# Sparse attention and a squared-ReLU MoE on one core: casting DMAs for batches 2 and 3, earlier hooks, late strided x through DRAM

## Chip, cores, metric

One NeuronCore of a Trainium2 chip. The metric is device microseconds (us) of one execution; medians are over the executions of one kernel. Times in a profile count from the start of the profiled execution's span, which is 1.5 to 2 us shorter than the reported time. "Batch" is one of 8 attention batches, "chunk" one of 9 blocks of 512 tokens of the MoE, "group" one step of the program's schedule: mostly four or eight large matmuls. A DMA is *issued* when an engine puts it into its queue, and has *landed* when its data are there; the *granted clock* is the share of TensorE's full clock in the profile's clock records. A run is called slow when it is over 1.5% above the fastest of its kernel; ratios use the other, fast, runs alone.

## The reference

```python
def _attn_ref(q, k, v):                       # q, k, v: (8, 8, 576, 64) float32
    scores = scale * np.matmul(q, k.transpose(0, 1, 3, 2))
    rel = pos[:, None] - pos[None, :]
    mask_local = (rel >= 0) & (rel < 32)                                    # heads 0..3
    mask_strided = (rel >= 0) & (pos[None, :] % 32 == pos[:, None] % 32)    # heads 4..7
    ...                                       # masked softmax
    return np.matmul(attn, v)

def _moe_ref(x, w_in, w_out):                 # x: (4608, 512), w_in: (512, 2048), w_out: (2048, 512)
    r = np.maximum(x @ w_in, 0.0)
    return (r * r) @ w_out

def reference(**kwargs):
    ...
    x = np.ascontiguousarray(attn_out.transpose(0, 2, 1, 3)).reshape(B * S, H * D)
    return _moe_ref(x=x, **moe_kwargs)
```

## The kernel before

The kernel writes the order of every engine's instructions itself. A list of MoE groups is walked through; before each group come as many attention steps as are due, then the *hooks* of that group: loads, casts and DMA transposes. A hook only gives the place of an instruction in its own engine's queue. Each engine then runs its queue in order, waiting only where data or buffers make it wait.

Batches 0 and 1 load with casting DMAs on GpSimd's queue, straight to bf16. Batches 2 and 3 load float32 on SyncE's queue and GpSimd casts. From batch 2 on, q and k of the strided heads (`q_d`, `k_d`) go by a casting DMA to DRAM and come back through a DMA transpose on SyncE's queue (`qT_s`, `kT_s`). From batch 4 on, the local heads' q and k are transposed by DMA too (`qT`, `kTl`).

```python
    def cast_str_dram(b):
        for name, src in (("q", q), ("k", k)):
            t = dram.tile([4 * SP_, NJ * D], BF16, name=f"{name}_d")
            nc.gpsimd.dma_start(
                out=t.rearrange("(x y) c -> x (y c)", x=16),
                in_=src[b, H // 2:H].rearrange("h (x y) d -> (h x) (y d)", x=4))
            big[b, name] = t

    def transpose_str(b):
        for name in "qk":
            o = strT.tile([128, NJ // 2, 4 * SP_], BF16, name=f"{name}T_s")
            nc.sync.dma_start_transpose(out=o, in_=big.pop((b, name)))
            ...

    def transpose_local(u):
        ...
            nc.sync.dma_start_transpose(out=dst.rearrange("c (t p) -> c t p", p=QL),
                                        in_=s[name].rearrange("p t h d -> p (t h d)"))

    def load_v_str_sw(b):          # strided v by one casting DMA, rows of 1024 bytes: not used before
        t = v_st.tile([SP_, 2, NJ * D], FP32, name="v_st")
        t = t.rearrange("p h c -> p (h c)").bitcast(BF16).rearrange("p (h c) -> p h c", h=4)
        nc.gpsimd.dma_start(out=t, in_=v[b, 4:8].rearrange("h (p j) d -> p h (j d)", j=NJ))
        ...

    def loads(b):                  # batches 2 and 3
        u = 4 * b
        for i in range(2):
            load_qk_local(u + i, nc.sync, gate=gates.get(b) if i == 0 else None)
        for i in range(2):
            load_v_local(u + i, nc.sync)
        load_v_str(u + 2, nc.sync)
        load_v_str(u + 3, nc.sync)
        if b >= XB:
            cast_str_dram(b)
        cast_qk_local(u, pool2)    # pool2: copies on GpSimd
        cast_qk_local(u + 1, pool2)
        cast_v_local(u)
        cast_v_local(u + 1)
        cast_v_str(u + 2)
        cast_v_str(u + 3)

    def plan(b, n0, g0, g1):
        if b < LB:                 # LB = 4
            at(n0, lambda: loads(b))
            if b >= XB:            # XB = 2
                at(n0 + (12 if b == 2 else 6), lambda: transpose_str(b))
            return
        g = g0 + (g1 - g0) * 45 // 100
        at(g, lambda: loads_qk(b))
        at(max(g + 8, g0 + (g1 - g0) * 8 // 10), lambda: transpose_str(b))
        at(n0, lambda: loads_v(b))
        for i in range(2):
            at(g + 14 + 4 * i, lambda u=4 * b + i: transpose_local(u))
    ...
    for n, g in enumerate(groups):
        while done < due[n]:
            steps[done]()
            done += 1
        for fn in hooks.get(n, ()):
            fn()
        g()
        tick()
```

The softmax here doesn't subtract the row's maximum and nothing guards it: scores larger than these inputs give would overflow.

## Time and profile before

| | before |
|---|---|
| time, median of 4 runs | 319.46 us (318.58 to 319.88) |
| span of the profiled execution | 317.8 us |
| TensorE busy | 299.0 us, 94% of the span |
| TensorE waits for a DMA over 0.5 us | none |
| granted TensorE clock | full throughout |

The main views (busy times, slices, windows by stage, TensorE's waits) are in the prediction. This is SyncE's queue in the timeline of the kernel before (start in us, time until the queue went on, line, operation, tiles):

```profile
60.09 3.31 SPq L171 DMA_TRANSPOSE kT_s<-k_d  x1
...
64.60 0.39 SPq L118 DMA_DIRECT2D q_st<-in_q_dram  x1
...
99.15 1.20 SPq L198 DMA_TRANSPOSE kTl<-k_l  x1
```

The first is batch 2's second strided transpose; the trace has it landed at 66.2 us, 6.1 us after its issue. Batch 3's first load follows it **in the same queue**, 4.5 us later. So before the change the order of the queue kept the next batch's float32 loads behind most of this transpose; what kept GpSimd's own copies of that batch back is shown below. The third is the first transpose of batch 4's local k: it is out at 99 us, while chunk 3, beside which batch 4 is worked, has its first relu square at 118.5 us.

### The profile page before, as it was taken

To read this page: it belongs to the slowest core of one execution; us is meant where nothing else is said; L and a number is where in the kernel's file an instruction comes from. 1 tells how busy PE (TensorE), PEld (TensorE's weight loads), DVE (VectorE), ACT (ScalarE), POOL (GpSimd) and SP (SyncE) were. 2 spreads that over 40 slices of the span, in tenths; PEclk is the share of its full clock that TensorE was granted. 3 is DMA by queue.
4 is the path that set the end of the run, shared out by engine and by line. 5 is a ranking of instruction groups with operands and counts; after the bars stand their busy time and mean duration, and the time that the engine had idled before them with its cause. 6 is when DMAs were issued, how large, how long until landed. Compare 5 with 4: busy or idle time off the path is not lost.

```text
span 317.8 us, 6089 instructions
## 1 busy us (share of the span) xinstructions
PE 299.0 (94%) x2319; PEld 147.7 (46%) x2362; DVE 162.1 (51%) x398; ACT 164.5 (52%) x339; POOL 82.7 (26%) x108
## 2 busy tenths in 40 slices
PE   7899699989899989999999999999999999999994
PEld 2543354445455444444444444544454444444441
DVE  5366653668656975756565557564465222222200
ACT  3757455777546765554555455545543344444311
POOL 8653113726730714642074034000000000000000
PEclk9999999999999999999999999999999999999999
DMA  8999969999997999999599775100421000000121
GB/s 157 176 206 204 189 111 251 217 268 223 210 174 170 196 215 175 215 219 203 130 223 240 149 185 93 40 24 26 54 71 48 35 33 35 33 33 35 54 78 66
DMA packets 87052, 43.41 MB, mean 137 GB/s; under 512 B 72112, under 2 KB 79984, under 8 KB 86832
## 3 DMA queue, kind: packets, MB, share of 16 engines
q1 hardware_dynamic: 73520, 31.86, 46.0%
q0 software_dynamic: 13504, 11.17, 23.2%
q8 instruction: 18, 0.29, 0.4%
q14 instruction: 10, 0.08, 0.1%
HBM read 37.08 MB, written 12.98 MB: 157 GB/s over the span
## 4 chain that ended last, share of the span: by engine, by line
PE 87%; DVE 5%; ACT 3%; issue 3%; POOL 1%; ACTq 0%; DVEq 0%; POOLq 0%
PE ph L472 35%; PE py L495 27%; PE ph L495 10%; PE pt L333 4%; PE pt L418 4%; ACT r L478 2%; PE pt L448 1%; DVE g_sb L481 1%; DVE xt L456 1%; PE pt L495 1%; ACT e L343 1%; DVE kTl L299 1%; PE pt L284 1%; PE pt L321 1%; PE pt L394 1%
## 5 line engine op out<-in xcount | busy, mean ns | idle before, releaser
L472 PE MATMUL ph<-xt,w_in_b 128*128 128x512 bf16 x549 | 141.4, 379 | 3.3 <-DVE xt L456 1.9
L478 ACT ACTIVATE r<-ph 128x512 bf16<-128x512 f32 x141 | 84.0, 598 | 100.5 <-PE ph L472 96.8
L481 DVE TENSOR_TENSOR g_sb<-r 128x512 bf16<-128x512 bf16 x144 | 67.6, 472 | 105.5 <-ACT r L478 105.0
L495 PE MATMUL py<-w_out_b,g_sb 128*128 128x512 bf16 x380 | 99.7, 379 | 1.6 <-issue 0.6
L495 PEld LDWEIGHTS <-g_sb 128*128 128x128 bf16 x576 | 52.8, 98 | 60.5 <-issue 3.1
L472 PEld LDWEIGHTS <-w_in_b 128*128 128x128 bf16 x576 | 51.6, 98 | 54.0 <-issue 0.8
L343 ACT ACTIVATE e<-pt 72x288 bf16<-72x288 f32 (+1 forms) x128 | 47.9, 407 | 14.4 <-PE pt L333 14.2
L495 PE MATMUL ph<-w_out_b,g_sb 128*128 128x512 bf16 x154 | 37.4, 379 | 0.3
L418 PEld LDWEIGHTS <-e 128*128 128x128 bf16 (+1 forms) x384 | 20.1, 97 | 15.4 <-issue 1.9
L217 POOL CAST vl<-vl_st 128x768 bf16<-128x768 f32 x12 | 10.8, 900 | 48.6 <-DMA vl_st<-in_v_dram 27.7
L431 DVE TENSOR_TENSOR x_s<-pt,rinv 72x384 bf16<-72x384 f32 (+1 forms) x36 | 18.3, 509 | 1.2
L431 DVE TENSOR_TENSOR x_l<-pt,rinv 96x384 bf16<-96x384 f32 x32 | 17.7, 553 | 1.1
L430 DVE RECIPROCAL rinv<-pt 96x6 f32<-96x6 f32 (+2 forms) x68 | 12.5, 184 | 10.6 <-PE pt L418 10.4
L349 DVE TENSOR_TENSOR e<-e,mask_str 72x576 bf16<-72x576 bf16 x28 | 14.7, 526 | 5.9 <-ACT e L343 5.6
L140 POOL CAST q_l<-q_st 96x768 bf16<-96x768 f32 x12 | 11.0, 917 | 25.0 <-DMA q_st<-in_q_dram 24.9
L499 ACT COPY y<-py 128x512 f32<-128x512 f32 x25 | 14.6, 586 | 4.0 <-PE py L495 4.0
L349 DVE TENSOR_TENSOR e<-e,mask_full 128x576 bf16<-128x576 bf16 x28 | 14.0, 501 | 1.6 <-ACT e L343 1.5
L499 ACT COPY y<-ph 128x512 f32<-128x512 f32 x10 | 5.8, 584 | 17.1 <-PE ph L495 17.1
L249 POOL CAST vs<-v_st 72x1024 bf16<-72x1024 f32 x12 | 13.7, 1159 | 1.2 <-DMA v_st<-in_v_dram 0.9
L140 POOL CAST k_l<-k_st 96x768 bf16<-96x768 f32 x12 | 11.2, 933 | 10.0 <-DMA k_st<-in_k_dram 7.6
L418 PE MATMUL pt<-vs,e 72*128 72x65 bf16 x192 | 11.7, 193 | 1.1 <-ACT e L343 1.1
L418 PE MATMUL pt<-vl,e 128*128 128x65 bf16 x192 | 10.8, 193 | 0.0
(100 smaller groups left out, 168.9 us busy)
## 6 DMA issues: line engine op xcount, KB each, us to landing
out_dram<-y SPq DMA_DIRECT2D x36, 256.0 KB, 2.2
vl_st<-in_v_dram SPq DMA_DIRECT2D x24, 144.0 KB, 2.9
v_st<-in_v_dram SPq DMA_DIRECT2D x12, 288.0 KB
q_st<-in_q_dram SPq DMA_DIRECT2D x16, 144.0 KB, 8.2
k_st<-in_k_dram SPq DMA_DIRECT2D x16, 144.0 KB, 5.1
w_out_b<-in_moe_w_out_dram POOLq DMA_DIRECT2D x4, 512.0 KB, 14.9
q_d<-in_q_dram POOLq DMA_DIRECT2D x6, 288.0 KB, 5.0
k_d<-in_k_dram POOLq DMA_DIRECT2D x6, 288.0 KB, 6.5
```

The costliest lines, as they stand in the source:

```text
L140: copy(t.rearrange("p j h d -> p h j d"), s[name + "f"].rearrange("p h (j d) -> p h j d", j=6))
L249: (copy or nc.gpsimd.tensor_copy)(t[:, :, 0:D], s["vf"].rearrange("p h (j d) -> p (h j) d", d=D))
L333: nc.tensor.matmul(pss[row][half][0:kn, w * i:w * (i + 1)], lhsT, rhs, start=u > 3, stop=True, skip_group_check=u < 4)
L343: nc.scalar.activation(e[0:kn, lo:lo + S // 2], pss[row][half][0:kn, 0:S // 2], AF.Exp, scale=scale)
L349: nc.vector.tensor_tensor(x, x, m, op=ALU.mult)
L418: nc.tensor.matmul(po[:, n - n0, :], e[0:kn, pos(n):pos(n) + 128], rhs[0:kn, src(n), 0:D + 1], start=True, stop=True)
L431: nc.vector.tensor_tensor(x, po[0:w, 0:m, 0:D], rinv[0:w, 0:m].to_broadcast([w, m, D]), op=ALU.mult)
L472: nc.tensor.matmul(ph, w_in_b[:, kk, 128 * ff:128 * (ff + 1)], xt[kk][:, 512 * c:512 * (c + 1)], start=(kk == order[0]), stop=(kk == order ...
L478: nc.scalar.activation(r, ph, AF.Relu)
L481: later(1, lambda: nc.vector.tensor_tensor(g[:, ff, :], r, r, op=ALU.mult))
L495: nc.tensor.matmul(py, g[:, ff, 128 * j:128 * (j + 1)], w_out_b[:, ff, :], start=(ff == 0), stop=(ff == 15))
L499: nc.scalar.copy(y, py)
```

## The change

The intent: load batches 2 and 3 as batches 0 and 1 are, without GpSimd's casts; queue batch 1's reorders two to four groups sooner; finish each batch's attention two groups before its chunk (14 for batches 6 and 7), so that the MoE does not wait for x; take the strided x of batches 6 and 7 through DRAM and a DMA transpose instead of TensorE; and halve the last block.

```diff
     XB = 2
+    XD = B - 2
@@ step_E
+        if not local and b >= XD:
+            xd = dram.tile([S, 2 * D], BF16, name="x_d")
+            nc.sync.dma_start(out=xd.rearrange("(p j) c -> p (j c)", j=NJ), in_=x.rearrange("p n d -> p (n d)"))
+            nc.sync.dma_start_transpose(out=xt[p][:, b * S:(b + 1) * S], in_=xd)
+            st.pop(u)
+            return
@@ mm2: last block in two halves of 256 columns
+        if c == NCH - 1 and j == 3:
+            ...
@@ loads
     def loads(b):
-        u = 4 * b
-        for i in range(2):
-            load_qk_local(u + i, nc.sync, gate=gates.get(b) if i == 0 else None)
         ... (float32 loads and GpSimd's casts, all removed)
+        load_qk_local_sw(b, (4 * b, 4 * b + 1))
+        cast_str_dram(b)
+        load_v_local_sw(b)
+        for u in (4 * b + 2, 4 * b + 3):
+            t = vss[v_slot(u)]
+            h = 2 * units[u][1]
+            for i in range(2):
+                nc.gpsimd.dma_start(out=t[:, NJ * i:NJ * (i + 1), 0:D],
+                                    in_=v[b, h + i].rearrange("(p j) d -> p j d", j=NJ))
+            st.setdefault(u, {})["v"] = t
@@ schedule
-    ready = {2: 56}
+    ready = {2: 58, **{b: starts[b] - (14 if b >= XD else 2) for b in range(3, B)}}
@@ plan
-            if b >= XB:
-                at(n0 + (12 if b == 2 else 6), lambda: transpose_str(b))
+            at(g0, lambda: transpose_str(b))
+            for i in range(2):
+                at(g1 + 2 * i, lambda u=4 * b + i: cast_qk_local(u, dve2, "q"))
+                at(g1 + 2 * i + 1, lambda u=4 * b + i: cast_qk_local(u, dve2, "k"))
             return
-        g = g0 + (g1 - g0) * 45 // 100
+        g = 50 if b == LB else g0 + (g1 - g0) * 45 // 100
@@ hooks
-    second(12, lambda: cast_qk_local(4, dve2, "q"))
-    second(13, T_(4, "q"), lambda: cast_qk_local(4, dve2, "k"))
     ...
+    second(10, lambda: cast_qk_local(4, dve2))
+    second(11, lambda: cast_qk_local(5, dve2))
     ...
-    plan(2, 18, 0, 0)
+    plan(2, 14, 28, 28)
-    plan(3, 34, 0, 0)
+    plan(3, 38, 48, 45)
```

Cut: weights of groups, order of steps within a batch (`stream_steps`), exponentials at once beside chunk 1's second layer, PSUM banks of chunk 0's first groups, `vl_st`'s memsets moved to group 50. With `g = 50` the loads of batch 4 come at group 50 instead of 42, and its local transposes (`g + 14`, `g + 18`) at groups 64 and 68 instead of 56 and 60.

More of the change, by code (lines that the diff above doesn't have):

```diff
@@ L260 @@
     clock = [0]
+    relaxed = [False]
     pending = []
@@ L468, in mm1 @@
         if kks[0] == order[0]:
-            phs[ff] = banks["pt"].pop(0) if pool == "pt" else bank(pool or "ph")
+            phs[ff] = banks["pt"].pop(0) if pool == "pt" else bank(pool[:2] if pool else "ph")
         ph = phs[ff]
@@ L479, in mm1 @@
         if c == 0 and 2 < ff < NP:
-            banks["pt"].insert(0, ph)
+            banks["pt"].append(ph)
         later(1, lambda: nc.vector.tensor_tensor(g[:, ff, :], r, r, op=ALU.mult))
@@ L487, in mm2 @@
         g = gs[c]
+        if c == NCH - 1 and j == 3:
+            if part % 2:
+                return
+            cols = slice(128 * part, 128 * part + 256)
+            py = bank(pool)[:, 0:256]
+            for ff in range(16):
+                nc.tensor.matmul(py, g[:, ff, 128 * j:128 * (j + 1)], w_out_b[:, ff, cols],
+                                 start=(ff == 0), stop=(ff == 15))
+            y = y_pool.tile([128, 512], FP32, name="y")
+            nc.scalar.copy(y[:, 0:256], py)
+            r0 = 512 * c + 128 * j
+            nc.sync.dma_start(out=out[r0:r0 + 128, cols], in_=y[:, 0:256])
+            return
         if part == 0:
@@ L505 @@
     T_ = lambda u, nm: (lambda: step_T(u, nm))
-    S_ = lambda u, at_once=False: (lambda: step_S(u, at_once))
+    S_ = lambda u, at_once=False: (lambda: step_S(u, at_once or relaxed[0]))
     D_ = lambda u, part: (lambda: step_D(u, part))
@@ L542, in stream_steps @@
     def stream_steps(lo, hi, base):
-        order = [T_(lo, "q"), T_(lo, "k"), T_(lo + 1, "q"), S_(lo), T_(lo + 1, "k")]
+        order = [T_(lo, "q"), T_(lo, "k"), T_(lo + 1, "q"), S_(lo), T_(lo + 1, "k"), lambda: None]
         ends = {}
@@ L547, in stream_steps @@
                 order.append(S_(u + 1))
+            if u < hi:
+                order.append(D_(u, 0))
             if u > lo:
@@ L551, in stream_steps @@
             if u < hi:
-                order.append(D_(u, 0))
                 if u + 2 < hi and has_T(u + 2):
@@ L562 @@
     pool2 = (nc.gpsimd.tensor_copy, nc.gpsimd.tensor_copy)
-    gates = {2: w_out_b[0:1, 12, 0:1]}
     def loads_1():
@@ L575, in loads_1 @@
         load_w_out(3)
-        for t in vl_sts:
-            nc.gpsimd.memset(t[0:32], 0.0)
     def loads(b):
-        u = 4 * b
-        for i in range(2):
-            load_qk_local(u + i, nc.sync, gate=gates.get(b) if i == 0 else None)
-        for i in range(2):
-            load_v_local(u + i, nc.sync)
-        load_v_str(u + 2, nc.sync)
-        load_v_str(u + 3, nc.sync)
-        if b >= XB:
-            cast_str_dram(b)
-        cast_qk_local(u, pool2)
-        cast_qk_local(u + 1, pool2)
-        cast_v_local(u)
-        cast_v_local(u + 1)
-        cast_v_str(u + 2)
-        cast_v_str(u + 3)
+        load_qk_local_sw(b, (4 * b, 4 * b + 1))
[8 more added lines that the diff above has]
+            st.setdefault(u, {})["v"] = t
     def loads_qk(b):
@@ L686, in add @@
                 starts[c] = len(groups)
-            groups.append(lambda: mm1(c, i))
-            weights.append(3 if c < 3 else 5)
+            groups.append(lambda: mm1(c, i, pool="pt free" if c == 0 and i < NP + 3 else None))
+            weights.append(4 if c == 1 else 3 if c < 3 else 5)
         else:
             groups.append(lambda: mm2(c, i, pool))
-            weights.append(7 if c < 2 else 5)
+            weights.append(6 if c < 2 else 5)
     def mm1_alone(c):
@@ L702 @@
     mm1_alone(1)
+    alone = range(len(groups), len(groups) + 15)
     for i in range(16):
@@ L722, in plan @@
             at(n0, lambda: loads(b))
-            if b >= XB:
-                at(n0 + (12 if b == 2 else 6), lambda: transpose_str(b))
+            at(g0, lambda: transpose_str(b))
+            for i in range(2):
+                at(g1 + 2 * i, lambda u=4 * b + i: cast_qk_local(u, dve2, "q"))
+                at(g1 + 2 * i + 1, lambda u=4 * b + i: cast_qk_local(u, dve2, "k"))
             return
-        g = g0 + (g1 - g0) * 45 // 100
+        g = 50 if b == LB else g0 + (g1 - g0) * 45 // 100
         at(g, lambda: loads_qk(b))
@@ L742 @@
     N_, O_ = (lambda u: lambda: step_N(u)), (lambda u: lambda: step_O(u))
-    second(12, lambda: cast_qk_local(4, dve2, "q"))
-    second(13, T_(4, "q"), lambda: cast_qk_local(4, dve2, "k"))
-    second(14, T_(4, "k"), lambda: cast_qk_local(5, dve2, "q"))
-    second(15, T_(5, "q"), lambda: cast_qk_local(5, dve2, "k"))
-    second(16, T_(5, "k"))
-    second(17, S_(4, True))
-    second(19, S_(5, True))
-    second(20, D_(4, 0))
-    second(21, D_(4, 1), ts("q", 0))
-    second(22, ts("q", 1), D_(5, 0))
-    second(23, E_(4), D_(5, 1))
-    second(24, ts("k", 0), ts("k", 1))
-    second(25, E_(5))
-    second(26, S_(6, True))
-    second(28, S_(7, True), N_(6))
+    second(10, lambda: cast_qk_local(4, dve2))
+    second(11, lambda: cast_qk_local(5, dve2))
+    second(12, T_(4, "q"), T_(4, "k"))
+    second(13, T_(5, "q"))
+    second(14, T_(5, "k"))
+    second(16, S_(4, True))
+    second(18, S_(5, True))
+    second(19, D_(4, 0))
+    second(20, D_(4, 1), ts("q", 0))
+    second(21, ts("q", 1), D_(5, 0))
+    second(22, E_(4), D_(5, 1), ts("k", 0))
+    second(23, ts("k", 1))
+    second(24, E_(5))
+    second(25, S_(6, True))
+    second(27, S_(7, True))
+    second(28, N_(6))
     second(29, O_(6))
@@ L760 @@
     second(31, O_(7))
-    plan(2, 18, 0, 0)
+    plan(2, 14, 28, 28)
     done_prev, g_prev = 0, 32
-    plan(3, 34, 0, 0)
+    plan(3, 38, 48, 45)
+    for t in vl_sts:
+        second(50, lambda t=t: nc.gpsimd.memset(t[0:32], 0.0))
     for b in range(2, B):
@@ L773 @@
     for n, g in enumerate(groups):
+        relaxed[0] = n in alone
         while done < due[n]:
```

## The prediction

> **What bounds the kernel now.** I read the page first: busy time, granted clock and the share of the DMA engines, slice by slice.
>
> ```profile
> PE 299.0 (94%) x2319; PEld 147.7 (46%) x2362; DVE 162.1 (51%) x398; ACT 164.5 (52%) x339; POOL 82.7 (26%) x108
> ...
> PEclk9999999999999999999999999999999999999999
> DMA  8999969999997999999599775100421000000121
> ```
>
> TensorE is busy nearly throughout, at full clock, and no other engine is above 52%. The DMA engines are full until about 200 us. So time can only be won by filling TensorE's gaps, by giving it less to do, or by shortening the last microseconds after it. Next I cut the span where the timeline of TensorE shows the MoE's parts change (first layer of chunk 0, its second layer, the same of chunk 1, first layer of chunk 2, then one stretch for each batch), and read the windows:
>
> ```profile
> 24.00:38.26 14.26, 11.05 (x69) 5.13 (x68) 9.24 (x28) 9.05 (x18) 4.43 (x7) 1.00 1.47 195
> 38.26:59.60 21.34, 19.98 (x220) 10.42 (x222) 10.32 (x24) 12.55 (x30) 6.07 (x9) 1.00 0.95 193
> 59.60:78.01 18.41, 17.10 (x151) 8.78 (x153) 13.21 (x28) 14.26 (x30) 9.49 (x11) 1.00 1.09 237
> 78.01:99.65 21.64, 20.17 (x236) 11.10 (x239) 13.63 (x37) 10.84 (x27) 10.18 (x12) 1.00 1.06 195
> 99.65:117.44 17.79, 16.57 (x137) 8.23 (x136) 15.22 (x34) 12.48 (x25) 6.54 (x8) 1.00 1.05 184
> 117.44:149.62 32.18, 31.66 (x252) 15.65 (x256) 20.21 (x47) 16.82 (x36) 14.48 (x16) 1.00 1.03 207
> ...
> 245.20:299.84 54.64, 54.34 (x249) 24.75 (x254) 13.22 (x32) 23.21 (x39) 0.00 (x0) 1.00 0.11 39
> ```
>
> Columns: window, length, then busy time of PE, PEld, DVE, ACT, POOL. Length minus the PE column is its idle time: 3.2, 1.4, 1.3, 1.5, 1.2, 0.5 us. The three windows left out idle 0.6, 0.6 and 0.4 us, the last shown 0.3. From 24 to 300 us TensorE idles only about 11 us. What it waits for, over the whole trace:
>
> ```profile
> PE pt L284 <- DVE q_l L140: 2.6, 2, 1.7
> PE ph L472 <- DVE xt L456: 1.9, 5, 1.1
> ...
> PE pt L333 <- DVE kTl L299: 1.2, 3, 0.7
> PE pt L418 <- ACT e L343: 1.1, 2, 1.0
> ...
> PE pt L381 <- ACT e L343: 0.6, 2, 0.4
> ...
> PE ph L472 <- ACT r L478: 0.5, 1, 0.5
> PE pt L381 <- ACT y L499: 0.4, 1, 0.4
> ```
>
> (total us, times, longest.) The first is batch 1's reorder of q on VectorE, ahead of the transposes of its local heads. The timelines of VectorE and GpSimd show why it is late:
>
> ```profile
> 31.99 1.45 DVE L140 COPY q_l<-q_st 96x768 bf16<-96x768 bf16 x1
> ...
> 36.47 0.35 DVE L140 COPY q_l<-q_st 96x768 bf16<-96x768 bf16 x1
> ```
>
> ```profile
> 31.80 1.43 POOL L577 MEMSET vl_st<- 32x768 f32 x2
> ```
>
> The same copy takes 0.35 us four microseconds later. The slow one ran exactly beside GpSimd's memsets.
>
> **What the Trainium skill says.** Perfetto Trace Analysis, section Identifying the Most-Contended Engine: matmul busy share is a poor measure of the distance to the limit, as matmuls are pipelined. This trace agrees: a 128x512 matmul is recorded as 379 ns, while 64 of them at the end start within 13.8 us, 216 ns apart. A gap therefore costs its idle time and about 0.16 us of pipeline tail (379 minus 216) on top. SBUF — State Buffer, section Who interferes with whom: copy and cast of VectorE in a two-port mode and GpSimd exclude each other, and the later one blocks. The 1.45 against 0.35 us agrees. DMA: Bandwidth & Descriptors, section SWDGE vs HWDGE vs iDMA: a cast during DMA can only be issued from GpSimd; here all casting loads are on GpSimd's queue. Same page, section Two DMAs through the same engine are not ordered: a DMA that reads what another wrote must be issued after the first one's completion semaphore. So the new way of late strided x is two latencies in series; this trace has it for q and k (casting copy to DRAM 5.0 and 6.5 us, transpose 5.0 and 4.5), not yet for x.
>
> **The change, part by part.** Numbers are TensorE's time.
>
> 1. Batch 1 sooner (24 to 38 us). Its four reorders are queued in MoE groups 10 and 11 instead of 12 to 15, the transposes from group 12; the memsets move to group 50. The two waits of 2.6 us in all go, with two tails of 0.16: 2.9. MoE groups 5 to 7 of chunk 0 take free banks of the larger pool, so the 0.5 us wait for ACT's relu goes: 0.7 with its tail. By group 10 the loads are there (issued at 14.6 and 15.8, landing after 12.1 and 12.4 us, so 26.7 and 28.2; group 10 is at about 28.4). VectorE must put four copies (about 0.35 to 0.53 us) between the squares, so I leave 0.3 us of a new wait. Saved: 3.3.
> 2. Batch 1's strided units (38 to 60 us). The scores of unit 7 come a group before the sums of unit 6 instead of in the same one: the 0.6 us for e go, with tails; the 0.4 us for y may stay. Saved: 0.8.
> 3. Batch 2 (60 to 100 us). An empty step gives the k copies a little time, exponentials go at once while ACT has no relus, the transposes of x come after the next unit's first products. Of 1.0 us for kTl and 1.1 us for e in these windows, with four tails 2.7 us in all, I take half: 1.3.
> 4. End of each batch. Steps end two groups before their chunk, 14 for batches 6 and 7. Two groups of four matmuls are 8 x 0.216 = 1.7 us, more than the longest xt wait of 1.1. The five waits go with tails: 1.9 + 5 x 0.16 = 2.7, of which I take 2.5, as a denser batch 3 may lag further.
> 5. Late strided x by DRAM. Four units lose eight transposes each. In the timeline such a block takes 0.26 us (from 115.46 to 115.72): 4 x 0.26 = 1.0. VectorE also loses four copies of 0.75 us, beside other work.
> 6. The last block. Its second half is 256 columns: the copy after the last matmul, now 0.59 us, should take about 0.37 and the last store is half as large: 0.4.
>
> Batches 2 and 3 by casting DMAs save no TensorE time themselves. They take 20 casts of 0.7 to 1.2 us off GpSimd, and give VectorE eight copies of 0.35 to 0.53 us, some 3.5 us beside other work, in stages where it is at 48% to 72% (10.3 of 21.3, 13.2 of 18.4).
>
> Sum of savings: 3.3 + 0.8 + 1.3 + 2.5 + 1.0 + 0.4 = 9.3. Against it I put 1.8 us for what the change tightens: batches 3 and 6 have 20 groups instead of 24 and 32 (VectorE is already at 86% from 99.7 to 117.4 us), and the extra copies. Net 7.5 us: 319.5 to **312.0 us**, 2.3% less.
>
> **The rivals.** (a) *A DMA wait in VectorE's queue.* The copies of batches 2 and 3 stand in order on VectorE; if their load has not landed, all of its work stops. Batch 2 joins the queue behind the output weights, whose last load lands at 46.3 us (31.05 + 15.3); the loads before land 1.5 to 1.8 us apart for this size, so q and k should be there at about 48 and 50, against some 50 and 51 when copied. Batch 3 is issued about seven groups of 1.1 us before its copy; alone on the engines such a load took 5.9 us. For it: margins of 0 to 2 us. Against: GpSimd waited little between issues in this stretch. If real, 1 to 4 us come back: 313 to 316. (b) *VectorE becomes the bound in the compressed batch 3.* Estimated from rows of this trace, its work there is some 20 us in about 22. For it: 86% already. Against: GpSimd's casts that slow it are partly gone, and the two groups of slack absorb a lag of 1.7 us. If real, 1 to 2 us come back: 313 to 314. (c) *The gaps were hidden time only in name*: moved steps make the same waits elsewhere, and only points 1, 5 and 6 stay: 4.7 us, 314.8. (d) *Better than my sum*: all of point 3, no new waits: 309.
>
> **Range and chances.** The line for 2% is 313.2, only 1.2 us above my figure. (d) sets the low side, (a) and (c) the high one: 309.3 to 315.8. Faster by over 2%: 0.67. Within 2%: 0.31. Slower by over 2% needs a stall of over 14 us, as from a load a whole stage late: 0.02.
>
> **What would show it.** Waits of TensorE after: no q_l row above 0.5 us, no xt row above 0.3 us; idle in the stretch that replaces 24 to 38 us below 0.6 us; the first layer of chunk 3 starting some 6 us before 117.4. VectorE's reorders at 0.35 to 0.55 us each. No VectorE wait for DMA over 0.5 us (rival a); if a row "DVE q_l" or "DVE k_l" waiting for q_st or k_st with 2 us or more appears, the prediction fails on that step. Strided x transposes on TensorE should fall from 12 blocks of eight to 8, and no wait for xt from a DMA before chunks 6 and 7. From the last matmul to the end: about 3.6 us instead of 4.

## The result, and the profile after

Ratios here and below are the mean time of one kernel's fast runs over the mean of the other's in the same rounds, so not quite the ratio of the medians quoted.

| | before | after |
|---|---|---|
| median | 319.46 us | 339.78 us (338.84 to 350.85; the run of 350.85 is slow) |
| ratio of fast runs | | 1.063 (95%: 1.0594 to 1.0666) |
| span of the profile | 317.8 us | 338.3 us |
| mean granted clock | 1.0 | 0.959 |

The change made the kernel 6% slower. The page of the kernel after, busy times and slices (answering the lines at the head of the prediction):

```profile
PE 306.6 (91%) x2346; PEld 150.8 (45%) x2346; DVE 155.3 (46%) x402; ACT 164.0 (48%) x340; POOL 76.3 (23%) x103
...
PEclk9999999976997858999999999999999999999999
DMA  8999999999999999999559898821122000100012
```

Two things are new in PEclk: dents in slices 9 and 10 and in 13 to 16, that is 68 to 85 us and 101 to 135 us. TensorE's busy time has *grown* by 7.6 us although the change gives it less to do. (Some 4 us of that is an estimate of mine for records: the trace before lacks 43 of its 2362 matmuls, this one none; a5 and a9 below, with the same matmuls, differ by 41 records and 4.1 us of busy time.) TensorE's waits, the largest rows:

```profile
PE pt L335 <- DMA kTl<-k_l: 13.1, 2, 11.4
PE pt L335 <- DMA kT_s<-k_d: 12.3, 2, 9.7
```

The rows for q_l and for xt ahead of the first layer, which the prediction showed, are gone. In their place are 25.4 us for two kinds of DMA transpose. In time order, from TensorE's timeline (start, length, and in brackets the idle time before it and what ended that):

```profile
77.43 0.70 PE L335 MATMUL pt<-qT_s,kT_s 64*72 64x72 bf16 x16 [9.69 <-DMA kT_s<-k_d]
...
102.12 0.70 PE L335 MATMUL pt<-qT_s,kT_s 64*72 64x72 bf16 x16 [2.59 <-DMA kT_s<-k_d]
...
123.90 0.66 PE L335 MATMUL pt<-qT,kTl 64*128 64x96 bf16 x12 [11.37 <-DMA kTl<-k_l]
124.49 3.60 PE L480 MATMUL ph<-xt,w_in_b 128*128 128x512 bf16 x8
...
129.93 1.89 PE L480 MATMUL ph<-xt,w_in_b 128*128 128x512 bf16 x8
```

They are batch 2's strided heads, batch 3's strided heads, batch 4's local heads. The last two lines are eight equal matmuls each: 3.60 us just after a wait, 1.89 us five microseconds later. The clock is at half after the wait. Ahead of the last microsecond the trace's clock records show it three times: half clock from 71.38 us for 10.24 us, from 102.10 for 3.41, from 115.75 for 13.65. TensorE was idle in the first and third until 77.43 and 123.90, so work at half clock was 4.2 + 3.4 + 5.5 = 13.1 us, which at full clock would have taken half of that: **6.5 us lost**. That is why busy time grew beyond what the missing records explain.

The windows of 20 us show the same by stage (columns as in the prediction; then granted clock, the packets' time as a share of the DMA engines', over 1 where packets of two queues overlap, GB/s). After:

```profile
20.00:40.00 20.00, 20.00 (x166) 10.22 (x164) 13.86 (x42) 13.05 (x27) 7.80 (x11) 1.00 1.40 199
40.00:60.00 20.00, 20.00 (x200) 10.03 (x198) 10.37 (x24) 13.27 (x28) 9.62 (x12) 1.00 1.57 162
60.00:80.00 20.00, 9.75 (x92) 4.90 (x92) 6.21 (x17) 7.11 (x18) 5.77 (x8) 0.78 1.49 128
80.00:100.00 20.00, 19.53 (x199) 10.35 (x196) 14.39 (x39) 11.60 (x27) 0.00 (x0) 0.96 1.89 93
```

And before:

```profile
20.00:40.00 20.00, 16.63 (x122) 8.04 (x123) 12.04 (x33) 11.27 (x21) 6.28 (x9) 1.00 1.41 198
40.00:60.00 20.00, 18.64 (x201) 9.83 (x204) 9.61 (x22) 11.76 (x29) 6.07 (x9) 1.00 0.92 193
60.00:80.00 20.00, 18.69 (x171) 9.54 (x173) 14.78 (x32) 15.38 (x33) 11.36 (x13) 1.00 1.12 233
80.00:100.00 20.00, 18.53 (x214) 10.33 (x217) 11.84 (x32) 9.86 (x25) 8.31 (x10) 1.00 1.01 193
```

Up to 60 us the change does what it was meant to do: TensorE has no idle time at all, where it had 3.4 and 1.4 us. From 60 us on the DMA engines are *more* occupied (1.49 and 1.89 against 1.12 and 1.01) and move *less* (128 and 93 GB/s against 233 and 193).

**A clock that doesn't tick with idle time.** VectorE squares each of the MoE's 144 relu blocks in order, 16 to a chunk, so the start of the first square of a chunk tells how far a kernel is. From the traces, before in us and the others as the difference to it ("v rows, early" and "old loads, early" are experiments below):

| first square of | before | after | v rows, early | old loads, early |
|---|---|---|---|---|
| chunk 1 | 61.30 | -4.8 | -4.9 | -4.9 |
| chunk 2 | 101.34 | +9.1 | -5.6 | -6.1 |
| chunk 3 | 118.48 | +23.9 | -6.2 | -3.5 |
| chunk 4 | 150.72 | +23.7 | -6.4 | -0.7 |
| chunk 6 | 215.09 | +23.8 | -6.3 | -0.6 |
| chunk 7 | 246.28 | +21.3 | -8.8 | -3.2 |
| last square | 299.80 | +21.3 | -8.8 | -3.2 |

All of the loss is between chunk 1 and chunk 3. Ahead of it the kernel after is 4.8 us *early*, behind it it wins another 2.6.

**Why the transposes are late: the queues.** SyncE's and GpSimd's queues in the kernel after:

```profile
52.72 8.43 SPq L172 DMA_TRANSPOSE kT_s<-k_d  x1
...
79.56 12.00 SPq L172 DMA_TRANSPOSE kT_s<-k_d  x1
...
93.07 5.94 SPq L112 DMA_DIRECT2D q_st<-in_q_dram  x2
...
119.62 1.22 SPq L199 DMA_TRANSPOSE qT<-q_l  x1
120.94 1.22 SPq L199 DMA_TRANSPOSE kTl<-k_l  x1
```

```profile
49.88 0.80 POOL L605 DMA_DIRECT2D vs<-in_v_dram  x1 [0.68 <-DMA k_st<-in_k_dram]
51.55 0.70 POOL L130 DMA_DIRECT2D q_st<-in_q_dram  x1 [0.86 <-PE pt L396]
...
55.31 0.53 POOL L164 DMA_DIRECT2D q_d<-in_q_dram  x1 [1.69 <-DMA vl<-in_v_dram]
```

The first `vs` line is the last load of batch 2; the next is the first load of **batch 3**, at 51.6 us, though its hook is group 38, far ahead of where TensorE was. Only buffers and earlier loads hold GpSimd's queue (here for under 2 us each, in brackets), not TensorE's groups: with its casts gone, GpSimd ran ahead. Before, batch 3's copy to DRAM went out straight after the last cast of batch 2:

```profile
61.91 2.29 POOL L249 CAST vs<-v_st 72x1024 bf16<-72x1024 f32 x2
64.16 0.49 POOL L163 DMA_DIRECT2D q_d<-in_q_dram  x1
```

After, batch 2's transposes were issued at 51.1 and 52.7 us, so they ran beside all of batch 3's casting loads. `kT_s`, issued at 52.7, landed at 77.4 us: 24.7 us against 6.1 before. One batch later the same: issued 79.6, landed 102.1, beside batch 4's `q_d` and `k_d` copies (issued 77.5 and 78.3) and the last loads of batch 3. In the packets from 54 to 99 us both queues have work all the time, and a 256-byte packet of a transpose takes 62 to 234 ns on average (stretches of 5 us), against 19 to 41 ns before. The loads suffer too: batch 3's `k_st`, issued at 52.9 us, took 22.0 us to land.

SyncE's queue pays once more. Each issue blocked it (8.43 and 12.00 us), so batch 4's loads, whose hook is also later now, started at 93.1 us (before: 81.0), and its local transposes, at groups 64 and 68 in place of 56 and 60, went out at 119.6 and 120.9 us, behind six loads of v and two transposes of x in the same queue, while TensorE had stood since 112.5 us.

### The profile page after: what moved, and what is told of

Read it like the earlier page. It is cut to its first block, busy times and chain, and to the rows that moved or that the text cites. A ratio compares the mean times of both kernels' runs of the same rounds, so it can differ in the third digit from the quotient of the medians.

```text
span 338.3 us, 6081 instructions
## 1 busy us (share of the span) xinstructions
PE 306.6 (91%) x2346; PEld 150.8 (45%) x2346; DVE 155.3 (46%) x402; ACT 164.0 (48%) x340; POOL 76.3 (23%) x103
## 4 chain that ended last, share of the span: by engine, by line
PE 68%; DMA 25%; SPq 3%; issue 1%; POOL 1%; ACT 1%; DVE 1%; POOLq 0%; ACTq 0%
PE ph L480 27%; PE py L516 25%; DMA k_d<-in_k_dram 7%; DMA kT_s<-k_d 7%; PE ph L516 4%; DMA w_out_b<-in_moe_w_out_dram 4%; DMA vl<-in_v_dram 4%; PE pt L335 3%; PE pt L420 3%; DMA vl_st<-in_v_dram 2%; PE py L535 2%; SPq L199 1%; PE pt L480 1%; DMA kTl<-k_l 1%; PE ph L502 1%
## 5 line engine op out<-in xcount | busy, mean ns | idle before, releaser
L480 PE MATMUL ph<-xt,w_in_b 128*128 128x512 bf16 x552 | 143.9, 387 | 0.0
L489 DVE TENSOR_TENSOR g_sb<-r 128x512 bf16<-128x512 bf16 x144 | 63.9, 444 | 129.8 <-ACT r L486 128.7
L516 PE MATMUL py<-w_out_b,g_sb 128*128 128x512 bf16 x400 | 102.8, 379 | 0.0
L345 ACT ACTIVATE e<-pt 72x288 bf16<-72x288 f32 (+1 forms) x128 | 45.8, 407 | 36.5 <-PE pt L335 36.5
L335 PE MATMUL pt<-qT_s,kT_s 64*72 64x72 bf16 x256 | 8.5, 209 | 12.4 <-DMA kT_s<-k_d 12.3
L218 POOL CAST vl<-vl_st 128x768 bf16<-128x768 f32 x8 | 7.4, 924 | 47.8 <-DMA vl_st<-in_v_dram 30.2
L432 DVE RECIPROCAL rinv<-pt 96x6 f32<-96x6 f32 (+2 forms) x68 | 12.6, 185 | 11.9 <-PE pt L420 11.6
L140 POOL CAST q_l<-q_st 96x768 bf16<-96x768 f32 x8 | 7.0, 879 | 44.6 <-DVE e L351 27.4
L335 PE MATMUL pt<-qT,kTl 64*128 64x96 bf16 x144 | 6.1, 210 | 12.1 <-DMA kTl<-k_l 11.4
L335 PEld LDWEIGHTS <-kT_s 64*72 64x72 bf16 x256 | 6.3, 120 | 19.4 <-DMA kT_s<-k_d 13.3
L335 PEld LDWEIGHTS <-kTl 64*128 64x128 bf16 x192 | 4.9, 96 | 20.8 <-DMA kTl<-k_l 14.1
```

Of the source, the lines that this page charges most:

```text
L218: nc.gpsimd.tensor_copy(t[:, :, :, 0:D].rearrange("p h t d -> p (h t) d"), s["vf"])
L335: nc.tensor.matmul(pss[row][half][0:kn, w * i:w * (i + 1)], lhsT, rhs, start=u > 3, stop=True, skip_group_check=u < 4)
L345: nc.scalar.activation(e[0:kn, lo:lo + S // 2], pss[row][half][0:kn, 0:S // 2], AF.Exp, scale=scale)
L432: nc.vector.reciprocal(rinv[0:w, 0:m], po[0:w, 0:m, D:D + 1])
L480: nc.tensor.matmul(ph, w_in_b[:, kk, 128 * ff:128 * (ff + 1)], xt[kk][:, 512 * c:512 * (c + 1)], start=(kk == order[0]), stop=(kk == order ...
L489: later(1, lambda: nc.vector.tensor_tensor(g[:, ff, :], r, r, op=ALU.mult))
```

## The experiments

Twelve kernels ran. In the quoted expectations the theories carry the numbers and letters that they had at that time; the text ahead of each quotation says what was to be told apart. Two are probes, which compute nothing. The first questions: is it that DMA transposes and casting loads slow each other by nature, or by the size of the rows, or is it another part of the change?

### m1_transpose_beside: what a transpose and a load cost each other

A probe in phases, each ended by a barrier: four DMA transposes of a 288x512 array alone; casting loads of several row sizes alone; both together.

```diff
+    phases = [[T], [rows128], [T, rows128], [rows768], [T, rows768], [rows1024], [T, rows1024], ...]
+    for ph in phases:
+        done = []
+        for fn in ph:
+            done += fn()
+        end(done)              # one VectorE copy from each destination, then a barrier of all engines
```

> A probe with a wrong result on purpose: it runs the disputed transfers by themselves, in phases with a barrier between them. One phase is four DMA transposes of 295 KB from DRAM alone; then each kind of load (casting with rows of 128, 768 and 1024 bytes on GpSimd's queue, plain with rows of 256 bytes on SyncE's, GpSimd's and ScalarE's queue) alone and with the four transposes beside it. Theory 1 (transposes and GpSimd's casting loads slow each other): a phase with transposes and 128-byte casting rows lasts at least 1.5 times the sum of the two alone, its 256-byte transpose packets take 70 ns and more against about 20 alone; the same beside 768-byte rows. Beside loads on SyncE's own queue it lasts about the sum. Theory 2 (the new loads are only more and smaller packets, nothing to do with transposes): each phase with both lasts the sum of the two alone within 15%. If the ScalarE queue's plain loads also slow the transposes, it is the second queue and not the cast.

Measured, in the probe's windows (transposes alone; 128-byte casting rows alone; the two together; 768-byte rows with transposes; 1024-byte rows with transposes; columns DVE, POOL, clock, DMA share, GB/s):

```profile
5.73:14.35 8.62, 0.49 (x4) 0.00 (x0) 1.00 0.74 137
14.79:30.05 15.26, 1.06 (x8) 12.80 (x16) 1.00 1.32 78
30.79:50.53 19.74, 1.48 (x12) 12.81 (x16) 1.00 1.93 120
60.46:76.29 15.83, 0.74 (x8) 2.66 (x4) 1.00 1.07 149
88.03:108.24 20.21, 0.73 (x8) 2.80 (x4) 1.00 1.12 117
```

Together 19.7 us, less than 8.6 + 15.3; 768-byte rows 15.8 against 8.6 + 9.1, 1024-byte rows 20.2 against 8.6 + 11.1. Beside plain loads on the queues of SyncE, GpSimd and ScalarE it was 18.4, 19.8 and 17.2 us, against sums of 21.2, 20.9 and 21.7. So the sum or less, but for half a microsecond at 1024 bytes. From the first issue to the end of the last 256-byte packet the four transposes took 8.0 us alone, and 13.4, 14.9 and 19.4 us beside rows of 128, 768 and 1024 bytes: 1.7 to 2.4 times as long (their packets 29 to 44 ns instead of 22). **No slowing beyond sharing** came out here, and the small rows were not the worst.

### a1_loads_before: the change without its casting loads

The loads of batches 2 and 3 as before, at the hooks of before; all else as changed, but that `vl_st`'s memsets stand at group 17 instead of 50.

```diff
-        load_qk_local_sw(b, (4 * b, 4 * b + 1))
-        ... (casting loads)
+        ... (loads(b) of before: float32 on SyncE's queue, casts on GpSimd)
-    plan(2, 14, 28, 28)
+    plan(2, 18, 28, 28)
-    plan(3, 38, 48, 45)
+    plan(3, 34, 48, 45)
```

> The changed kernel with one part undone: batches 2 and 3 are loaded as before (plain loads on SyncE's queue, casts on GpSimd, same places), all else of the change kept. If the casting loads of batches 2 and 3 are the cause of all that was lost (theory 1 and 2 alike): no wait of TensorE for kT_s or kTl over 1 us, granted clock 1.0, 309 to 314 us. If the later loads of batch 4 (hook 50) cause the 11.4 us wait for kTl by themselves: that wait stays and the time is 322 to 330.

Fast runs 324.82, 322.52 and 324.39 us, ratio 1.0147 (1.0087 to 1.0206), mean clock 0.98. The casting loads account for some 15 us of the 20; something else in the change costs more than the change wins. The profile of this kernel fell in a stray execution of 790 us, in which TensorE is busy for 782.7 us and waits for no DMA; it isn't used, so which waits a1 had in its other runs was not seen.

### a2_v_rows: strided v in rows of 1024 bytes

Four casting DMAs with 128-byte rows become one with 1024-byte rows and two copies on GpSimd.

```diff
-        for u in (4 * b + 2, 4 * b + 3):
-            ... (four casting DMAs into vs)
+        load_v_str_sw(b)
+        cast_v_str(4 * b + 2)
+        cast_v_str(4 * b + 3)
```

> The changed kernel with the strided v of batches 2 and 3 loaded in one casting DMA each with rows of 1024 bytes and copied into place on GpSimd, instead of four with rows of 128 bytes; the rest of the casting loads stays. Theory 1 (interference with transposes): the casting loads still stand beside the transposes, 3,000 of some 5,300 small packets of a batch remain, so part of the wait stays: 322 to 336 us. Theory 2 (number of small packets): the load shrinks by 44% of the small packets and the waits for kT_s fall by half or more: 315 to 325.

319.84 us median, ratio 0.9999 (0.9931 to 1.0068). No wait for `kT_s` is left; for batch 4's local transposes it is:

```profile
PE pt L335 <- DMA kTl<-k_l: 7.6, 2, 5.3
```

This looked as if the small rows were the cause. It was a **confounded** experiment: GpSimd's two copies wait for the load of `v_st`, so GpSimd issued batch 3's first load only at 59.0 us, after batch 2's transpose had landed (58.7). Row size and overlap had changed together.

### a3_gate3: batch 3's loads only after batch 2's transpose

Rows left at 128 bytes; one element is copied on GpSimd from batch 2's `kT_s` into the buffer that batch 3's q goes to, ahead of that load.

```diff
             t = qk_st.tile([QL, 2, 6 * D], FP32, name=f"{name}_st")
+            if b == 3 and name == "q":
+                nc.gpsimd.tensor_copy(t[0:1, 0, 0:1], st[10]["kT"][0:1, 0, 0:1])
```

> The changed kernel with one instruction more: GpSimd waits for batch 2's transposed k before it issues batch 3's casting loads, so that these no longer stand beside batch 2's transposes. Theory 1: batch 2's transposes land by about 62 us instead of 77 and the 9.7 us wait goes; batch 3's copies and batch 3's own transposes come later or stay slow beside batch 3's v, so a wait of 3 to 12 us appears there: 322 to 338. Theory 2 (only the volume): the same bytes and packets have to move, starting later, so the time is that of the changed kernel or longer: 338 to 348.

328.28 us (326.36 to 331.09), ratio 1.0291: 11.5 us better than after. Its waits:

```profile
PE pt L337 <- DMA kTl<-k_l: 11.5, 2, 10.1
PE pt L337 <- DMA kT_s<-k_d: 4.0, 1, 4.0
```

Batch 2's wait is gone. Batch 3's transposes are now the slow ones (SyncE's queue held 11.71 us from 72.8 us), beside batch 4's `q_d` and `k_d` copies at 71.5 and 72.2 us. The gate has moved the collision on by one batch, and the local transposes of batch 4 still cost 11.5 us.

### m2_mixture: the kernel's own mixture of DMAs, in a probe

The order of the kernel around 48 to 60 us: two transposes, v in 128-byte rows, q and k, two DRAM-to-DRAM copies, local v, v again; and the same with one kind left out or exchanged.

```diff
+    phases = [..., [T2, R(0, 2), Q(0, 2), C(2), L(1), R(2, 4)],      # as in the kernel
+              [T2, W(0, 1), Q(0, 2), C(2), L(1), W(1, 2)],           # 1024-byte rows
+              [T2, R(0, 2), Q(0, 2), L(1), R(2, 4)],                 # no copies
+              [T2, R(0, 2), C(2), L(1), R(2, 4)],                    # no q and k
+              [T2]]
```

> A probe with a wrong result on purpose, as m1_transpose_beside: phases with barriers. In order: four casting copies from DRAM to DRAM alone, and beside four transposes; two local v loads (128-byte rows) alone, and beside four transposes; then the changed kernel's own sequence between batch 2 and batch 3 (four strided v loads with 128-byte rows, two q/k loads with 768-byte rows, two casting copies to DRAM, local v, four strided v) alone; the same with two transposes beside it; with strided v in rows of 1024 bytes; without the casting copies; without the 768-byte loads; two transposes alone. Theory 1' (what slows the transposes is a particular neighbour): one of the last phases with transposes ends its second transpose 8 us or more sooner than the full sequence does. Theory 2' (a transpose shares the DMA engines packet by packet, and every neighbour takes its share): the second transpose ends 8 to 14 us after its start in all of them, against about 5 alone, and the length of a phase is about the sum of its parts; then the 25 us of the kernel need something that the probe lacks.

From the start of the transposes to the landing of the second: 8.8 us in the full mixture, 18.6 with 1024-byte rows, 9.3 without the copies, 8.6 without q and k, 5.0 alone. (Earlier phases had four transposes beside the copies alone, 14.2 us, and beside local v alone, 15.0; alone they took 8.0 in m1.) Leaving a kind of load out changed little, so no one kind was to blame. The kernel's own mixture gives 1.8 times the time alone, not the kernel's factor of four; the phase with 1024-byte rows comes near it, 3.7 times, with 256-byte packets of up to 199 ns (stretches of 2 us). In that phase the first casting load went out 0.3 us ahead of the transposes, in the others 0.2 to 0.5 us behind them. Whether this order matters, or GpSimd's queue being already full when the transposes start, stays open. The kernel's trace gives a hint only: the 16 parts of such a transfer end in a clump and a few stragglers. Of the last `vs` load, 13 parts were done by 57.3 us, the others at 60.8, 64.4 and 67.8.

### a5_v_rows_early4: 1024-byte rows, and batch 4's local transposes earlier

a2, and one line more: batch 4's local transposes at groups 57 and 59 instead of 64 and 68.

```diff
-            at(g + 14 + 4 * i, lambda u=4 * b + i: transpose_local(u))
+            at(g + (7 + 2 * i if b == LB else 14 + 4 * i), lambda u=4 * b + i: transpose_local(u))
```

> As a2_v_rows (strided v of batches 2 and 3 in rows of 1024 bytes), and the DMA transposes of batch 4's local q and k stand 7 and 9 groups after its loads instead of 14 and 18, so before batch 4's v loads and before the transposes of batch 3's x in SyncE's queue. Theory A (their place in the queue makes the 5.3 and 2.3 us waits for kTl): both waits go, clock 1.0, 307 to 312 us. Theory B (the DMA engines are too full at that time, wherever they stand in the queue): the waits stay or move to another DMA, 317 to 322 us.

310.15 us (309.52 to 310.68), ratio **0.9719** (0.9687 to 0.9751): faster than before by 2.8%. The hooks of these transposes are worth 9.7 us against a2 (on another chip; the medians of before differ by 0.2 us there). TensorE's largest waits:

```profile
PE pt L335 <- ACT e L345: 1.3, 2, 0.7
PE py L535 <- DVE xt L627: 1.3, 1, 1.3
```

No wait for a DMA among the large rows, and full clock. Of the 9.6 us of span won (317.8 to 308.2), 6.6 are idle time (18.8 to 12.2) and 3.0 busy time (296.0; this trace lacks 41 matmul records, before 43, so by the estimate above both idle times are some 4 us too high). `kT_s` of batch 2, issued 53.0, landed 59.2, and GpSimd was held meanwhile:

```profile
57.33 2.40 POOL L250 COPY vs<-v_st 72x1024 bf16<-72x1024 bf16 x2 [11.88 <-DMA v_st<-in_v_dram]
59.67 0.68 POOL L130 DMA_DIRECT2D q_st<-in_q_dram  x1
```

For 11.9 us GpSimd waited for its own load before it could issue batch 3's. Whether the rows or this hold saved the kernel is still not told apart.

### a7_early4: the changed kernel with the early local transposes alone

The one line of a5, on the kernel after.

> The changed kernel with only batch 4's local transposes earlier (the other half of a5). With the four strided v loads of 128-byte rows as in the changed kernel, the waits for kT_s of 9.7 and 2.6 us stay. Theory A: the 11.4 us wait for kTl falls to under 3 us, 322 to 330 us. Theory B: it stays, 336 to 341 us.

335.58, 339.81, 334.02 and 328.12 us. Three are counted as slow, being over 1.5% above the fastest, so there is no ratio; the profile of the 335.58 us run shows why it scatters:

```profile
PE pt L335 <- DMA kT_s<-k_d: 19.6, 2, 10.9
```

The wait for `kTl` (11.4 us after) is gone, and the strided transposes cost more instead: batch 2's took from 51.7 to 78.7 us, batch 3's from 82.4 to 108.9. The early hooks alone don't mend the kernel: its fastest run, 328.1 us, is still 9 us slower than before. While both causes stand, one hides part of the other.

### a8_before_early4: old loads with the early local transposes

a1 and the same line.

> As a1_loads_before (batches 2 and 3 loaded as in the kernel before), and batch 4's local transposes earlier as in a5. Theory A: the time that a1 lost (324 at a granted clock of 0.98) was the wait for kTl, and it goes: 309 to 314 us, clock 1.0. Theory B: 322 to 325 us as a1.

314.61 us (313.11 to 315.82), ratio 0.9844 (0.98 to 0.9888). This is just above theory A's 309 to 314 us. Against the 324.4 us of a1's fast runs (median) the line is worth 9.8 us, as against a2: **the second cause is shown twice**, each time by that one line. And a8 is 4.5 us slower than a5, run on the same chip: the casting loads, with the hooks and memsets that go with them, do save time where they don't collide. The table above places it: at chunk 2 both are about 6 us ahead of before; a8 loses 2.6 by chunk 3 and 2.8 by chunk 4. Its largest wait is

```profile
PE pt L420 <- DVE x_l L433: 2.4, 1, 2.4
```

with 0.8 us each for GpSimd's two casts into `vl` behind it. Half clock follows this wait too, from 118.44 us for 3.41 us; by the 2.8 us of work in it that cost 1.4 us of the profiled run.

### a9_small_rows_gates: 128-byte rows, but no overlap

To part rows from overlap: a7 with the gate of a3, and a second gate of the same kind, so that batch 4's casting copies wait for batch 3's `kT_s`. All rows as in the change.

```diff
+            if b == 3 and name == "q":
+                nc.gpsimd.tensor_copy(t[0:1, 0, 0:1], st[10]["kT"][0:1, 0, 0:1])
 ...
+        if b == 4:
+            nc.gpsimd.tensor_copy(gate_t[0:1, 0:1], st[14]["kT"][0:1, 0, 0:1])
```

> As a7_early4 (the changed kernel, strided v still in four loads with 128-byte rows, batch 4's local transposes earlier), and GpSimd waits twice for a landed transpose: for batch 2's k before it issues batch 3's loads, for batch 3's k before it issues batch 4's casting copies to DRAM. So no casting load of the next batch stands beside a batch's transposes. Theory O (overlap: the transposes are slow because the next batch's casting loads share the DMA engines with them): the waits for kT_s fall from 19.6 us in all (a7) to under 5, time 309 to 317 us, although the rows are still small. Theory R (rows of 128 bytes themselves): waits of 8 us or more stay, 322 us or more.

310.31 us (309.07 to 313.51), ratio 0.9748 (0.9688 to 0.9809), full clock, and a single DMA wait of TensorE, 0.8 us. GpSimd's two gates and the load between them:

```profile
61.22 0.18 POOL L130 CAST q_st<-kT_s 1x1 f32<-1x1 bf16 x1 [10.16 <-DMA kT_s<-k_d]
61.77 0.70 POOL L133 DMA_DIRECT2D q_st<-in_q_dram  x1 [0.38 <-POOL q_st L130]
...
81.71 0.18 POOL L616 CAST gate_t<-kT_s 1x1 f32<-1x1 bf16 x1 [10.94 <-DMA kT_s<-k_d]
```

Batch 2's `kT_s` took from 53.0 to 61.1 us, batch 3's from 72.1 to 81.7. GpSimd stands for 21 us, and the kernel is some 24 us faster than a7 by the medians (another chip, and a7 scatters, but its fastest run is still 18 us above). Small rows do no harm once the transposes don't share with the next batch's loads.

### a10_v_rows_no_hold: 1024-byte rows, with overlap

The other corner: a5, with the two copies of v on VectorE (at groups 38 and 39, 62 and 63), so that GpSimd isn't held.

```diff
         load_v_str_sw(b)
-        cast_v_str(4 * b + 2)
-        cast_v_str(4 * b + 3)
+        for i in range(2):
+            at((38 if b == 2 else 62) + i, lambda u=4 * b + 2 + i: cast_v_str(u, nc.vector.tensor_copy))
```

> As a5_v_rows_early4, but the copies of the strided v stand on VectorE, later, so that GpSimd is no longer held by them between batch 2's loads and batch 3's (in a5 GpSimd issued batch 3's loads at 59.7 us, after batch 2's transposes had landed; in the changed kernel at 51.6). The rows of v are 1024 bytes as in a5. Theory O: batch 3's loads again stand beside batch 2's transposes, a wait for kT_s of 4 us or more comes back, 315 to 330 us. Theory R: the rows were the cause, and the time stays within 2 us of a5's 310.

321.33 us (320.49 to 323.7), ratio 1.0084 (1.0041 to 1.0128): 11 us worse than a5 by the medians (another chip), from 2.8% faster than before to 0.8% slower. The wait is back:

```profile
PE pt L335 <- DMA kT_s<-k_d: 10.2, 1, 10.2
```

and so is the overlap, on GpSimd's and on SyncE's queue:

```profile
47.22 0.67 POOL L130 DMA_DIRECT2D q_st<-in_q_dram  x1 [1.89 <-DMA w_out_b<-in_moe_w_out_dram]
```

```profile
53.02 14.79 SPq L172 DMA_TRANSPOSE kT_s<-k_d  x1
```

Batch 3's first load went out at 47.2 us, and `kT_s` landed at 77.8 us, 24.8 us after its issue, nearly as in the kernel after. **a9 and a10 settle it: without the overlap with the next batch's casting loads the wait is gone at either row size, and with it the wait is there at either.** My reading of a2 falls. The rows may still bear on the size of the loss: with overlap, the small rows (a7) stand 24 us above a9, the large ones (a10) 11 us above a5. No run parts this from the other things that differ there.

### a11_best_x_pe: a5 with the late strided x on TensorE

```diff
-    XD = B - 2
+    XD = B
```

> a5_v_rows_early4 with one part of the change undone: the strided x of batches 6 and 7 is transposed on TensorE again (32 transposes), not by way of DRAM. The prediction gave this part 1.0 us of TensorE's time: 1.0 us more than a5, 311.2. If its attention was not on the path there, 310.2 as a5; if its DMAs had cost a wait, less than a5.

311.70 us (311.51 to 311.79), ratio 0.977. The way through DRAM is worth about 1.5 us by the medians (a5 ran on another chip; the medians of before differ by 0.35 us there, and the intervals of the two ratios just overlap). The last square comes 1.9 us later than in a5, all of it between chunks 6 and 7.

### a12_best_whole_tail: a5 with the last block whole

```diff
-        if c == NCH - 1 and j == 3:
+        if False:
```

> a5_v_rows_early4 with the last output block in one piece again. The prediction gave the split 0.4 us: 310.6. If loading the weights twice for 256 columns costs what the shorter end saves: 310.2.

311.01 us (310.06 to 311.49), ratio 0.9747. By the medians the halves are worth 0.9 us, but the intervals of the two ratios overlap. The traces are firmer: from the end of TensorE's last matmul to the end of the span it is 3.2 us with halves and 3.7 without.

## Why the prediction was wrong

**Its sum of savings came out in the mended kernels, in part by luck; its account of what the change adds to the DMA queues failed.** By its own steps:

1. *Batch 1 sooner, 3.3 us.* Right. At the last square of chunk 0, a5 and the kernel after are 3.4 and 3.2 us ahead of before. The reorders took 0.34 to 0.49 us each, and no q_l row is left.
2. *Strided units of batch 1, 0.8 us.* Right or somewhat more: at chunk 1's first square 4.8 to 4.9 us are won, 4.1 foretold.
3. *Batch 2, 1.3 us,* and 4. *end of each batch, 2.5 us.* In the kernel after these were buried. The xt rows ahead of the first layer are gone in both. In a5, chunk 3 begins 6.2 us early where the prediction said some 6, but 4.9 of that was won by chunk 1. From there to the last square a5 wins 3.9 us, of which a11 gives 1.9 to step 5. So 3 and 4 together gave some 2.0 us of their 3.8.
5. *Late strided x, 1.0 us.* The 12 blocks of eight transposes fell to 8 as foretold; the size was too small, 1.5 to 1.9 us (a11).
6. *Last block, 0.4 us.* The end after the last matmul is 0.6 us shorter (a12).

(Its line for 2% is 313.1 us, 0.98 of 319.46, and not 313.2; nothing hangs on it.)

So a5 and a9 stand at 310.2 and 310.3 us, 9 us below before, close to the prediction's sum of 9.3 ahead of its allowance. That sum is right because steps that gave more than foretold (2, 5, 6) made up for 3 and 4; and a5 and a9 are not the kernel predicted, but that kernel with both faults taken out. The step that failed is rival (a), as the prediction put it: "Batch 3 is issued about seven groups of 1.1 us before its copy". By the windows of before that puts the issue near 66 us. It was at 51.6 us. I had read hooks as times, while buffers and earlier loads alone hold GpSimd's queue, not TensorE's groups: what had slowed it was the very work that the change took away. The page of before puts the idle time ahead of its casts down to loads, 27.7 us to `vl_st` and 24.9 to `q_st`; I read POOL's 26% and went no further. The prediction's "GpSimd waited little between issues in this stretch" fits that trace badly: GpSimd stands 13.3 us ahead of batch 2's gate at 46.5 us and up to 4.8 us ahead of a cast. Rival (a) then looked for trouble in one place, VectorE's copies of q and k. No row of VectorE waiting for a load showed. The trouble was the *transposes* that now shared the DMA engines with loads a batch ahead: 12.3 us of waits for `kT_s`, shown by a9 against a7 and by a10 against a5.

A second term is missing altogether: **batch 4's chain**. The diff moves its loads from group 42 to 50, its local transposes from 56 and 60 to 64 and 68, while batch 3 ends two groups earlier and TensorE has no more gaps. Slack that I never counted was used up from both ends: 13.1 us of waits for `kTl` in the kernel after, and about 10 us by a1 to a8 and a2 to a5.

A third: the prediction counts a wait as its idle time and 0.16 us of pipeline. Three of the waits cost 6.5 us more through the clock. The Trainium skill states this, and I had not taken it up: TensorE: Matmul & The Clock Gate, section HAM oscillation, says that a DMA wait that crosses a window of some 3.4 us throttles TensorE to half clock, so that the work after it starts slow. The trace agrees: the three records at half clock are 10.24, 3.41 and 13.65 us long, all multiples of 3.41 us, and each begins in or at the end of a DMA wait.

The books: 25.4 us of waits and 6.5 of half clock are 31.9 us. The kernel after and a5 differ by 21.3 + 8.8 = 30.1 us at the last square. The loss was thus some 30 us against gains of some 9.

Two sentences of the prediction were wrong in a way that didn't decide. "Batches 2 and 3 by casting DMAs save no TensorE time themselves": a5 against a8 says 4.5 us, hooks and memsets included. And "a stall of over 14 us, as from a load a whole stage late: 0.02" named the very thing that came about, with far too small a chance for a change that reorders three batches' traffic on in-order queues.

What stays open is the size: sharing gives a factor of about two in m1 and in most of m2, the kernel shows four (24.7 us against 6.1). Only m2's phase with 1024-byte rows comes near (18.6 us against 5.0). The state of the queues when the transposes start is my guess; no run isolates it.

## What to carry to other kernels

A hook in a program's order is a place in one engine's queue and not a time: when a change frees an engine that issues DMAs, ask how far it will now run ahead, and with what its loads will then share the DMA engines. Keep a transfer that TensorE waits for apart from loads that nobody needs yet; a one-element copy as a gate, at 0.2 us and GpSimd's idleness, was worth more than ten microseconds here. When gaps go and ends move forward, follow each later chain of DMAs to its use again, and count a wait of some 2.4 us or longer with its clock: half clock followed waits of 2.4 (a8) and 2.6 us here.

## What the Trainium skill lacked or had wrong

- DMA: Bandwidth & Descriptors, section Rules for kernel authors, says of two transposing streams that they must be serialized, and that "A transpose next to ordinary DMAs needs nothing". That rule is about right results, and those were right in every kernel (the probes compute nothing); but the time did suffer: `kT_s` took 24.7 us beside the next batch's casting loads, 6.1 before, 8.1 behind a gate.
- The same page, section Queues, rings and completion order, has each DMA engine alternate between queues packet by packet. A sharing of about two is my estimate from that, and the probe shows it (8.8 against 5.0 us). It doesn't account for the kernel's factor of four, nor for the 18.6 us of one probe phase. And I found no page that says that a transpose holds its issuing queue longer where it shares the engines: 8.43, 12.00 and 14.79 us, against 2.91 and 3.31 before.
- TensorE: Matmul & The Clock Gate puts the danger at idle gaps of more than about 3.4 us. Here 2.59 us of waiting was enough: the 3.41 us ahead of the drop at 102.10 us held 0.84 us of work, and the clock went to half. The starts of the three half-clock records lie a multiple of 3.41 us apart; on that grid the window from 132.82 us, with 1.90 us of work, was not followed by a drop. Both in the windows of the kernel after:

```profile
98.69:102.10 3.41, 0.84 (x4) 0.19 (x2) 0.75 (x2) 0.58 (x1) 0.00 (x0) 1.00 1.10 89
132.82:136.23 3.41, 1.90 (x13) 0.69 (x10) 2.47 (x8) 1.79 (x3) 1.66 (x2) 1.00 0.73 79
```

Where the edge lies is not shown: on the grids of their own records, 1.46 us of work in a window was followed by half clock in a8, 1.44 us was not in a7.
